# Loads of a cached-attention kernel split into two transfers of 64 partitions each

## The chip, the cores and the metric

The kernel runs on one core of one Trainium2 chip. The metric is the device time of one execution in microseconds (us), as the median of several runs; a profiled execution is one more run, of which a trace was taken. A core has a matrix engine (PE, with its weight loads shown as PEld), a vector engine (DVE), a scalar engine (ACT), GpSimd (POOL) and a sync engine (SP). SP issues the transfers between the chip's main memory (DRAM in the names) and the on-chip memory of 128 partitions; 16 DMA engines carry them out.

## What is computed

One token passes through two layers, each made of an attention block over a cache of keys and values and a mixer block, with a layer norm ahead of each. Both layers use the same weights and the same cache. Cut to what matters:

```python
def _A_ref(x, k_cache, v_cache, wq, wo):          # x: 1 x 1 x 640, 32 heads of 192
    q = (x @ wq).reshape(B, Sq, Hq, Dh).transpose(0, 2, 1, 3)
    k = k_cache[:, :, Sk - W:, :]                 # the last W = 4096 rows of 32768
    v = v_cache[:, :, Sk - W:, :]
    p = softmax(einsum("bhqd,bhkd->bhqk", q, k) * Dh ** -0.5)
    return einsum("bhqk,bhkd->bhqd", p, v).transpose(0, 2, 1, 3).reshape(B, Sq, Hq * Dh) @ wo

def _B_ref(x, w1, w2, w3, w4):                    # with one token the shifted part is zero
    x1 = x + hs
    return x1 + gelu(layernorm(x1) @ w3) @ w4

x = x + _A_ref(layernorm(x), ...)
x = x + _B_ref(layernorm(x), ...)
x = x + _A_ref(layernorm(x), ...)
x = x + _B_ref(layernorm(x), ...)
```

Everything is bfloat16. For one head, K and V are 4096 x 192 values each, 1536 KB. With a single token, every weight and cache value is used once per layer, so the work is mostly the moving of bytes: 218.5 MB are read in one execution.

## The kernel before

The 32 heads of a layer are taken in eight groups of four (`GROUPS`, L78), layer 1 from the last group to the first and layer 2 from the first to the last. For a head, `load_k` (L116) and `load_v` (L121) each bring 1536 KB into one cell: partition p gets 32 consecutive rows of the cache, 12,288 bytes in one run. `load_wo` (L137) brings the 960 KB of the output weights that belong to one group, 7,680 bytes to a partition. There are 11 cells (L72) of this size. `take` (L103) hands out the cell that has been free longest and `give` (L108) returns it when its last reader has been written into the program.

K has to be turned by DVE (`transpose_quart`, L305, instruction at L322) before PE can form the scores (`scores_quart`, L365). Layer 1 keeps the turned K of heads 0 to 6 in seven cells (`NKEEP`, L72), and layer 2 uses them without loading them again. Layer 1 also keeps half of V of head 3 (`VKEEP`, L74). In layer 2, a kept cell is given back when its head's scores are done (L511). V is read by `pv` (L450), wo by `out_proj` (L474).

The engines' order is the order in which the program is written (L89). Loads are put into one list beforehand (`layer_stream`, L174): while the V of one group comes in, the K of the next comes in turn with it, then the group's wo. SP issues the list in that order, each issue at the point where the framework's waits allow it. `need` (L210) runs the list forward as far as the load that is wanted. An issue waits for two kinds of things: for the last reader of the cell it writes, and for one of eight completion semaphores that the framework uses in turn, so that a transfer waits for the landing of the one eight places before it. Every load that is larger than a few bytes spans all 128 partitions; the last two V loads of a layer and its last wo are cut in two along the row.

The turn between the layers goes as follows. The last group of layer 1 ends at its output projection, the mixer follows with w3 (`load_w3`, L146) and w4 (`load_w4`, L154), and then attention of layer 2 begins with the scores of the kept heads 0 to 3. The V loads of heads 0 to 2 of layer 2 are issued while layer 1's mixer runs. The first K load of layer 2 is that of head 7, the next is that of head 8.

Of the kernel before, what the change touches and what calls it, by code (L numbers as in the profile page):

```python
# [17 lines left out]
P = 128  # L18
# [15 lines left out]
def kernel(  # L34
# [14 lines left out]
    nc = tc.nc  # L49
    _, _, D = A_x.shape  # L50
    _, H, Sk, Dh = A_k_cache.shape
# [9 lines left out]
    QH = 4  # L61
# [7 lines left out]
    s0 = Sk - W  # L69
# [2 lines left out]
    NKEEP, NCELL = 7, 11  # L72

    VKEEP, VHALF = 3, FREE // 2  # L74

    W3C, W4C = FREE // F, FREE // D
    assert W4C % 2 == 1 and W4C < NF
# [25 lines left out]
    def take(key):  # L103
        i = free.popleft()
        cell_of[key] = i
        return cells.tile([P, FREE], BF16, tag=f"cell{i}", name=f"cell{i}")
# [4 lines left out]
    def load_x():  # L111
        x_bf = const.tile([ND, P], BF16, name="x_bf")
        nc.sync.dma_start(x_bf[:], A_x.rearrange("a b (n p) -> (a b n) p", p=P))
        return x_bf

    def load_k(layer, h):  # L116
        t = take(("k", layer, h))
        nc.sync.dma_start(t[:], A_k_cache[0, h, s0:Sk, :].rearrange("(p j) d -> p (j d)", p=P))
        return t

    def load_v(layer, h):  # L121
        t = take(("v", layer, h))
        src = A_v_cache[0, h, s0:Sk, :].rearrange("(p j) d -> p (j d)", p=P)
        n = 2 if h in GROUPS[layer][-1][-2:] else 1
        step = FREE // n
        if (layer, h) == (1, VKEEP):
            n, step = 2, VHALF
        for i in range(n):
            if (layer, h, i) != (1, VKEEP, 0):
                nc.sync.dma_start(t[:, i * step:(i + 1) * step], src[:, i * step:(i + 1) * step])  # L130
        return t

    def load_wq(layer, kc):
# [3 lines left out]
    def load_wo(layer, c):  # L137
        t = take(("wo", layer, c))
        src = A_wo[c * QC:(c + 1) * QC, :].rearrange("(p c) n -> p (c n)", c=NA)
        n = 2 if c == GROUPS[layer][-1][0] // QH else 1  # L140
        step = NA * D // n
        for i in range(n):
            nc.sync.dma_start(t[:, i * step:(i + 1) * step], src[:, i * step:(i + 1) * step])
        return t

    def load_w3(layer):  # L146
# [7 lines left out]
    def load_w4(layer):  # L154
# [15 lines left out]
        return blocks  # L170

    LOADERS = {"x": load_x, "k": load_k, "v": load_v, "wq": load_wq, "wo": load_wo, "w3": load_w3, "w4": load_w4}

    def layer_stream(layer):  # L174
# [580 lines left out]
```

## Time and profile before

| What | Value |
|---|---|
| Median of three runs | 540.65 us (540.53 to 542.11) |
| The profiled execution's own time | 540.19 us |
| Its span, first to last instruction | 538.4 us |
| Read from DRAM | 218.53 MB, 406 GB/s over the span |
| PE busy | 281.0 us, 52% of the span |
| PEld busy | 229.0 us, 43% |
| DVE busy | 257.5 us, 48% |
| ACT busy | 54.7 us, 10% |
| Chain that ended last | DMA 71%, PE 14%, DVE 11%, issue 2%, ACT 1% |
| One issue on SP | 0.33 us |

The profile's page first gives busy times per engine, then cuts the span into 40 equal slices: in the rows of digits, 9 means busy for 90% of a slice or more, and PEclk is the clock that PE was granted, in tenths. The row of GB/s says what the DMA engines moved in each slice. The chain of waits is followed back from the last instruction, at each step to what released it; a DMA entry in it lasts from a transfer's issue to its landing, which includes the time that it stood behind earlier transfers. A table of windows gives for each stretch of time the busy time of PE, PEld, DVE, ACT and POOL with their instruction counts, the granted PE clock, the DMA engines' busy share and GB/s. DMA issues are listed with their size and the time from issue to landing.

### The profile page before, as it was taken

To read this page: it belongs to the slowest core of one execution; us is meant where nothing else is said; L and a number is where in the kernel's file an instruction comes from. 1 tells how busy PE (TensorE), PEld (TensorE's weight loads), DVE (VectorE), ACT (ScalarE), POOL (GpSimd) and SP (SyncE) were. 2 spreads that over 40 slices of the span, in tenths; PEclk is the share of its full clock that TensorE was granted. 3 is DMA by queue.
4 is the path that set the end of the run, shared out by engine and by line. 5 is a ranking of instruction groups with operands and counts; after the bars stand their busy time and mean duration, and the time that the engine had idled before them with its cause. 6 is when DMAs were issued, how large, how long until landed. Compare 5 with 4: busy or idle time off the path is not lost.

```text
span 538.4 us, 14866 instructions
## 1 busy us (share of the span) xinstructions
PE 281.0 (52%) x6820; PEld 229.0 (43%) x6820; DVE 257.5 (48%) x494; ACT 54.7 (10%) x249; POOL 2.0 (0%) x11
## 2 busy tenths in 40 slices
PE   0146546365363644545535676665454653636555
PEld 0045445254253533434425665554343543524434
DVE  2187536455455546546303147565363654545511
ACT  1001010010100101001201012010010101001011
POOL 1000000000000000000000000000000000000000
PEclk9999999999999999999999996555555555555555
DMA  8999999999999999999999999999999999999992
GB/s 351 429 422 422 419 427 421 422 424 420 421 422 425 420 422 420 421 423 425 401 401 406 345 380 424 421 421 420 424 421 424 423 420 422 424 421 424 422 408 98
DMA packets 23697, 219.48 MB, mean 408 GB/s; under 512 B 2516, under 2 KB 2900, under 8 KB 8148
## 3 DMA queue, kind: packets, MB, share of 16 engines
q1 hardware_dynamic: 23636, 218.54, 97.8%
q8 instruction: 53, 0.87, 0.7%
q14 instruction: 8, 0.07, 0.0%
HBM read 218.53 MB, written 0.00 MB: 406 GB/s over the span
## 4 chain that ended last, share of the span: by engine, by line
DMA 71%; PE 14%; DVE 11%; issue 2%; ACT 1%; SPq 0%; DVEq 0%; ACTq 0%
DVE cell_4809 L322 6%; DMA cell_567<-in_A_k_cache_dram 6%; DMA cell_1665<-in_A_v_cache_dram 5%; DMA cell_1053<-in_A_k_cache_dram 5%; DMA cell_2029<-in_A_k_cache_dram 5%; DMA cell_2517<-in_A_k_cache_dram 5%; DMA cell_3006<-in_A_k_cache_dram 5%; DMA cell_7424<-in_A_k_cache_dram 5%; DMA cell_5960<-in_A_k_cache_dram 5%; DMA cell_7917<-in_A_v_cache_dram 5%; DMA cell_6448<-in_A_k_cache_dram 5%; DMA cell_6936<-in_A_k_cache_dram 5%; PE O_ps L459 4%; DMA cell_3466<-in_A_k_cache_dram 4%; PE ST_ps L372 3%; DMA cell_8110<-in_A_wo_dram 3%
## 5 line engine op out<-in xcount | busy, mean ns | idle before, releaser
L372 PE MATMUL ST_ps<-Qblk,cell_200 128*128 128x4 bf16 x1200 | 45.6, 167 | 72.5 <-DVE cell_200 L322 72.5
L372 PE MATMUL ST_ps<-Qblk,cell_4809 128*128 128x4 bf16 x1200 | 45.3, 167 | 64.8 <-DVE cell_4809 L322 64.3
L463 DVE STREAM_TRANSPOSE o_sb<-O_ps 128x192 f32<-128x192 f32 x64 | 24.5, 383 | 113.0 <-PE O_ps L459 113.0
L459 PEld LDWEIGHTS <-PT 128*1 128x1 bf16 x2048 | 68.1, 114 | 22.8 <-issue 11.5
L372 PEld LDWEIGHTS <-cell_200 128*128 128x128 bf16 x1200 | 38.6, 105 | 85.3 <-DVE cell_200 L322 83.7
L372 PEld LDWEIGHTS <-cell_4809 128*128 128x128 bf16 x1200 | 38.5, 105 | 78.5 <-DVE cell_4809 L322 76.1
L472 ACT ACTIVATE oT<-oT_ps,rl 32x6 bf16<-32x6 f32 x64 | 16.5, 257 | 282.9 <-PE oT_ps L471 282.9
L408 ACT ACTIVATE Pr<-ST_ps,nb_sb,sc 128x32 bf16<-128x32 f32 x64 | 25.1, 487 | 0.5
L471 PE MATMUL oT_ps<-o_sb,Lq 128*32 128x6 f32 x128 | 16.9, 204 | 11.8 <-DVE o_sb L463 11.7
L339 PE MATMUL qT_ps<-xc,wq_sb 128*128 128x1 bf16 x480 | 15.8, 166 | 13.4 <-DMA wq_sb<-in_A_wq_dram 12.9
L339 PEld LDWEIGHTS <-wq_sb 128*128 128x128 bf16 x480 | 15.0, 105 | 14.1 <-DMA wq_sb<-in_A_wq_dram 13.6
L471 PEld LDWEIGHTS oT_ps<-o_sb,Lq 128*32 128x32 f32 x128 | 11.9, 141 | 20.6 <-issue 15.3
L417 PEld LDWEIGHTS <-Eq 128*32 128x32 bf16 x256 | 4.1, 105 | 31.1 <-DVE y_acc L522 25.3
L353 PE MATMUL Qrep_ps<-Xq,Lb 128*128 128x24 bf16 (+1 forms) x18 | 3.2, 180 | 24.7 <-DVE Xq L346 24.4
L408 ACT ACTIVATION_READ_ACCUMULATOR Pr<-ST_ps,nb_sb,sc 128x1 f32 x64 | 14.2, 222 | 0.0
L404 ACT COPY nb_sb<-nb_ps 128x4 f32<-128x4 f32 x16 | 2.6, 162 | 113.7 <-PE nb_ps L402 113.7
L422 PE MATMUL l_ps<-lpart,ones 128*128 128x4 f32 x32 | 9.4, 366 | 5.3 <-ACT PT L420 5.3
L346 DVE TENSOR_TENSOR Xq<-qT_ps,maskq 128x24 bf16<-128x24 f32 (+1 forms) x18 | 2.8, 155 | 19.5 <-PE qT_ps L339 19.4
L422 PEld LDWEIGHTS l_ps<-lpart,ones 128*128 128x128 f32 x32 | 8.0, 313 | 6.9 <-ACT PT L420 6.7
L402 PE MATMUL nb_ps<-dg,ones 4*128 4x4 f32 x32 | 9.0, 348 | 1.1
L402 PEld LDWEIGHTS nb_ps<-dg,ones 4*128 4x128 f32 x32 | 7.9, 307 | 1.9
L417 PE MATMUL PT_ps<-Pr,Eq 128*32 128x32 bf16 x256 | 5.3, 192 | 6.0 <-ACT Pr L408 5.8
(266 smaller groups left out, 469.2 us busy)
## 6 DMA issues: line engine op xcount, KB each, us to landing
wq_sb<-in_A_wq_dram SPq DMA_DIRECT2D x5, 1536.0 KB, 10.9
cell_198<-in_A_k_cache_dram SPq DMA_DIRECT2D x1, 1536.0 KB, 21.8
cell_256<-in_A_k_cache_dram SPq DMA_DIRECT2D x1, 1536.0 KB, 24.9
cell_317<-in_A_k_cache_dram SPq DMA_DIRECT2D x1, 1536.0 KB, 25.8
cell_371<-in_A_k_cache_dram SPq DMA_DIRECT2D x1, 1536.0 KB
cell_462<-in_A_k_cache_dram SPq DMA_DIRECT2D x1, 1536.0 KB, 30.2
cell_565<-in_A_v_cache_dram SPq DMA_DIRECT2D x1, 1536.0 KB, 30.3
cell_567<-in_A_k_cache_dram SPq DMA_DIRECT2D x1, 1536.0 KB, 30.3
```

The lines of the kernel that those rows point to most:

```text
L322: nc.vector.transpose(Tu, Ku[:, :, q * NY:(q + 1) * NY])
L339: nc.tensor.matmul(qT_ps[:, tl:tl + 1], lhsT=wq_sb[:, kc, t * P:(t + 1) * P], rhs=xc[:, kc:kc + 1], start=(kc == 0), stop=(kc == ND - 1))
L353: nc.tensor.matmul(Qrep_ps[:], lhsT=Lb[:], rhs=held["x"][:].rearrange("p t b -> p (t b)"), start=True, stop=True)
L372: nc.tensor.matmul(ST_ps[:, hq, q * ng + g, :], lhsT=T4[:, g, f, :, t], rhs=Qblk[:, h * NCOL + 2 * f + t, :], start=(n == 0), stop=(n == N ...
L402: nc.tensor.matmul(nb_ps[:], lhsT=ones[0:n, :], rhs=held["dg"][0:n, :], start=True, stop=True)
L408: nc.scalar.activation(out=Pr[:, hq].rearrange("p m g -> p g m"), in_=ST_ps[:, hq], func=ACTF.Exp, bias=nb_sb[:, hq:hq + 1], scale=sc[:, 0 ...
L417: nc.tensor.matmul(PT_ps[32 * m:32 * (m + 1), :, j, :], lhsT=Eq[:, j, :], rhs=held["Pr"][:, :, m, :], start=True, stop=True)
L422: nc.tensor.matmul(l_ps[:], lhsT=ones[:], rhs=held["l"][:], start=True, stop=True)
L459: nc.tensor.matmul(O_ps[r:r + 1, :], lhsT=PT[:, hq, i:i + 1], rhs=V[:, i * Dh:(i + 1) * Dh], start=(i < 4), stop=(i >= NB - 4))
L463: nc.vector.transpose(o_sb[:], O_ps[:].rearrange("p (a c) -> p c a", c=NA))
L471: nc.tensor.matmul(oT_ps[r, :], lhsT=Lq[:], rhs=o_sb[:, :, 0], start=True, stop=True)
L472: nc.scalar.activation(oT[r, :], oT_ps[r, :], ACTF.Copy, scale=rl[r, 0:1])
```

## The change

`load_k`, `load_v` and `load_wo` no longer issue their transfers themselves but through a new function, `start`. With `short` set, it issues two transfers, of partitions 0 to 63 and of partitions 64 to 127, one right after the other on the same queue; otherwise it issues one as before. `short` is set in layer 2 (`layer == 1` in the code) for heads under 12, that is, for K and V of the first three groups, and for those groups' wo. The bytes, the cells, the order of the loads and the instructions of the other engines stay. A run in a partition is as long as before; a half has 64 of them, four for each of 16 DMA engines, where a whole load has eight.

```diff
     VKEEP, VHALF = 3, FREE // 2
+    SHORT = 12
...
+    def start(dst, src, short):
+
+        n = P // 2 if short else P
+        for p in range(0, P, n):
+            nc.sync.dma_start(dst[p:p + n], src[p:p + n])
+
     def load_k(layer, h):
         t = take(("k", layer, h))
-        nc.sync.dma_start(t[:], A_k_cache[0, h, s0:Sk, :].rearrange("(p j) d -> p (j d)", p=P))
+        start(t[:], A_k_cache[0, h, s0:Sk, :].rearrange("(p j) d -> p (j d)", p=P), layer == 1 and h < SHORT)
         return t
...
             if (layer, h, i) != (1, VKEEP, 0):
-                nc.sync.dma_start(t[:, i * step:(i + 1) * step], src[:, i * step:(i + 1) * step])
+                start(t[:, i * step:(i + 1) * step], src[:, i * step:(i + 1) * step], layer == 1 and h < SHORT)
         return t
...
         for i in range(n):
-            nc.sync.dma_start(t[:, i * step:(i + 1) * step], src[:, i * step:(i + 1) * step])
+            start(t[:, i * step:(i + 1) * step], src[:, i * step:(i + 1) * step], layer == 1 and c * QH < SHORT)
         return t
```

## The prediction

> **What bounds the kernel now.** I read the page's slices first, then its table of DMA queues, the chain of waits in order of time, and then a table of windows over the part that the change touches.
>
> ```profile
> PEclk9999999999999999999999996555555555555555
> DMA  8999999999999999999999999999999999999992
> GB/s 351 429 422 422 419 427 421 422 424 420 421 422 425 420 422 420 421 423 425 401 401 406 345 380 424 421 421 420 424 421 424 423 420 422 424 421 424 422 408 98
> ...
> q1 hardware_dynamic: 23636, 218.54, 97.8%
> ```
>
> One slice is 538.4 / 40 = 13.46 us. The 16 DMA engines are busy from the first slice to the last but one, at 420 to 425 GB/s, and the one hardware queue q1 carries 97.8% of all engine time. The exceptions are the start, the end and slices 20 to 24 (401, 401, 406, 345, 380), the turn from layer 1 to layer 2.
>
> ```profile
> 295.37 0.25 issue
> 295.62 0.57 PE mean_ps L275 x2
> ...
> 316.81 3.45 DVE cell_4809 L322 x4
> ...
> 357.83 0.81 PE y_ps L482 x30
> 358.66 26.15 DMA cell_5960<-in_A_k_cache_dram
> ...
> 391.56 25.38 DMA cell_6448<-in_A_k_cache_dram
> ...
> 423.68 25.18 DMA cell_6936<-in_A_k_cache_dram
> ...
> 486.03 25.91 DMA cell_7917<-in_A_v_cache_dram
> ...
> 511.96 15.97 DMA cell_8110<-in_A_wo_dram
> 527.98 0.57 PE y_ps L482 x15
> ...
> 535.95 0.28 DVE o_fin L723
> ```
>
> From 295 to 358 us the chain runs over PE and DVE; from 358.66 on it is made of K and V loads, and only 8 us of arithmetic stand behind the last wo load. That compute stands in the chain from 295 to 358 doesn't make it the limit there: the next table says what the DMA does meanwhile.
>
> ```profile
> 283.00:296.00 13.00, 7.81 (x192) 7.01 (x193) 4.30 (x17) 2.20 (x10) 0.00 (x0) 1.00 1.02 403
> 296.00:309.00 13.00, 8.74 (x293) 8.49 (x294) 1.78 (x10) 0.76 (x4) 0.00 (x0) 1.00 0.96 350
> 309.00:323.00 14.00, 10.72 (x290) 9.16 (x291) 5.54 (x13) 2.26 (x11) 0.00 (x0) 1.00 0.99 377
> 323.00:358.00 35.00, 23.39 (x572) 18.76 (x564) 23.23 (x41) 4.79 (x23) 0.00 (x0) 0.56 1.01 422
> 358.00:500.00 142.00, 73.48 (x1793) 59.77 (x1791) 74.77 (x130) 13.39 (x64) 0.00 (x0) 0.50 1.01 422
> ```
>
> The last column is GB/s. From 323 on the DMA moves 422 GB/s without a gap, during the compute stretch too: it works ahead. So a microsecond of DMA time added anywhere after the turn stands in the end time, except what falls into the turn's own gaps. Those are 13 x (1 - 350/422) + 14 x (1 - 377/422) = 2.2 + 1.5 = 3.7 us between 296 and 323.
>
> [...] Every large transfer of the kernel before spans 128 partitions, so no row of its trace shows a half[...].
>
> **The change, part by part.** *Which loads.* Layer 2 doesn't load K for heads 0 to 6, which are kept transposed. The short loads are K of heads 7 to 11 (5 x 1536 KB), V of heads 0 to 11 (11 x 1536 + 768 KB, half of head 3 being kept) and wo of three groups (3 x 960 KB): 20 loads, 28,224 KB = 28.90 MB. At 422 GB/s that is 68.5 us of DMA time, from about 291 us, when the first V load gets its turn, to about 362, with the full-width K loads of heads 12 to 15 among them. On the other engines the instruction order is unchanged; on SP 20 issues become 40.
>
> *Issues.* 20 more at 0.33 us (the length of one on SP in the timeline) are 6.6 us of SP, over a stretch in which SP mostly waits. The second half's issue follows the first's, behind 1.9 us or more of transfer. Cost 0; if an engine ran dry at each, at most 6.6.
>
> *Landings.* Each half adds one packet per engine that raises the semaphore. The trace's DMA records give 9 ns for it: 20 x 9 ns = 0.2 us. The runs keep their 12 KB.
>
> *In flight.* The framework turns eight completion semaphores: a ninth transfer waits for the first. Before, that is eight loads; the landing times show it, with 28 to 31 us in the steady part, eight times 1536 KB / 422 GB/s = 3.7 us.
>
> ```profile
> cell_4807<-in_A_k_cache_dram SPq DMA_DIRECT2D x1, 1536.0 KB, 9.2
> ...
> cell_5472<-in_A_k_cache_dram SPq DMA_DIRECT2D x1, 1536.0 KB, 17.5
> ...
> cell_5861<-in_A_k_cache_dram SPq DMA_DIRECT2D x1, 1536.0 KB, 24.0
> ```
>
> In the short region landing takes 9 to 24 us, so free cells are what limits there at first. Eight halves are four loads, 15 us. SP will wait on semaphores earlier, and behind it only later issues are queued[...]. An engine still has up to seven halves, 13 us, behind the one in work. Cost 0; at most a few us if the slowest engine falls far behind.
>
> *Rate.* [...] In the records of semaphore increments around 280 us the 16 engines finish one load within 4.4 us, in two clusters of eight about 2 us apart, and inside a cluster many differ by 0.05 to 0.4 us. [...] Bounds: 1.0 (the engine's own rate is the limit[...]) and 2.0. I take 1.9[...]: 68.5 x 0.9 = 61.7 us.
>
> *What is given back.* With the engines at half pace the first V loads last until the next cells are free, so the turn's gaps close: -3.7 us. First arithmetic of layer 2 hardly waits: its V loads, issued at 286 to 295, are first read at 315.
>
> *Sum.* +61.7 - 3.7 + 0.2 = +58. The profiled execution took 540.19 us with a span of 538.4, 0.5 under the median of 540.65. It would become 598.4; against the median, 598.9. I say 598. Compute is no second limit: behind slower loads it has more time.
>
> **Rivals.** *Ports have room.* The engine's own 26.4 GB/s (422 / 16) binds, and halves run as fast as wholes. [...] Time 540.9, up to 545 if the smaller window lets engines run dry.
>
> *Half out of step.* [...] Factor 1.4: 68.5 x 0.4 - 3.7 = +24, 564. [...]
>
> *Faster.* [...] Its whole price is the 3.7 us of gaps, 537[...]. Against: both halves wait for the same cell, and that cell's release is what is late.
>
> *Worse than half.* [...] 610 and over. Nothing in the profile speaks for it.
>
> **How the numbers follow.** Likeliest, factor 1.7 to 2.0 (585 to 606 us): 0.64. Half out of step, 1.15 to 1.7 (547 to 585): 0.18. Ports have room: 0.10, of which 0.06 within 0.3% and 0.04 slower. Faster: 0.04. Worse than half: 0.04. About 0.3%, 1.6 us, is what a measurement here can tell from no change. Slower is 0.64 + 0.18 + 0.04 + 0.04 = 0.90. The range 555 to 608 takes all of the likeliest and most of the second; outside are the two cases without loss, the weak end of the second and the worst.
>
> **What would show it.** In the slices, some nine figures, from slice 20 or 21 of a longer span on, should fall to 215 to 260 GB/s with the DMA digit still at 9: engines busy but slow. The packets' time in q1 rises while the bytes stay. The chain from about 310 to 420 should be made of K and V loads in place of PE and DVE, with landings of 25 to 30 us for halves of 768 KB. After the last half the rate is 422 again and the last load is followed by the same 8 us. The prediction is wrong if the rate stays near 420 in the halves, and its reason is wrong if the time is lost with the DMA digit below 9.

## The result and the profile after

The changed kernel takes 617.78 us as the median of four runs (613.52 to 620.9), against 540.87 us before (540.53 to 542.11, four runs, one more than in the table above). The ratio is 1.141, 95% interval 1.133 to 1.150: 77 us more. The direction, the place and the halving of the rate were forecast; the size, +58 us with a range up to 608 us, was too small. The profiled execution took 620.14 us with a span of 618.0. PE was granted about half its clock in the last part of the profiled execution before and the full clock in this one, but that isn't the difference: other executions of the kernel before took 539.2 to 542.3 us at the full clock and 540.7 to 541.7 us at the lower one.

The page's slices and its row for the hardware queue, one slice being 618.0 / 40 = 15.45 us:

```profile
DMA  8999999999999999999999999999999999999992
GB/s 356 427 423 423 421 424 422 423 423 422 423 421 423 422 421 423 403 408 350 214 219 229 222 223 227 218 214 215 213 296 421 421 423 421 424 420 426 418 401 84
...
q1 hardware_dynamic: 23956, 218.54, 98.1%
```

The digits are 9 in all slices but the first and the last, as before. But for ten slices the same busy engines move 213 to 229 GB/s, about half of what they move elsewhere. The bytes of the queue are the same 218.54 MB, in 23,956 packets against 23,636: 320 more, 16 for each of the 20 added transfers.

The chain of waits, in order of time (start, length, what):

```profile
320.45 16.71 DMA cell_4990<-in_A_k_cache_dram
...
337.23 29.15 DMA cell_5290<-in_A_k_cache_dram
...
393.08 40.77 DMA cell_5785<-in_A_k_cache_dram
433.91 29.12 DMA cell_5980<-in_A_k_cache_dram
...
607.58 0.57 PE y_ps L489 x15
...
615.56 0.28 DVE o_fin L730
```

Between 320 and 358 us arithmetic stood here before; now it is K loads, with one wo load from 366 to 393 us among the later ones. Behind the last load stand 8 us of arithmetic, as before. So the difference is in the loads.

The table of windows, whose last column is GB/s:

```profile
283.00:296.00 13.00, 6.40 (x140) 5.41 (x140) 4.12 (x15) 2.22 (x10) 0.00 (x0) 1.00 1.08 299
296.00:309.00 13.00, 5.67 (x177) 5.43 (x178) 1.07 (x8) 0.30 (x2) 0.00 (x0) 1.00 1.01 215
309.00:323.00 14.00, 8.03 (x255) 7.88 (x255) 1.44 (x6) 0.97 (x5) 0.00 (x0) 1.00 1.00 220
...
320.00:380.00 60.00, 27.86 (x674) 21.90 (x671) 20.97 (x42) 5.58 (x26) 0.00 (x0) 1.00 1.02 225
...
400.00:456.00 56.00, 15.53 (x376) 12.39 (x377) 16.56 (x28) 2.79 (x13) 0.00 (x0) 1.00 1.01 215
460.00:590.00 130.00, 67.40 (x1612) 54.58 (x1613) 68.00 (x117) 13.03 (x61) 0.00 (x0) 1.00 1.01 422
...
288.00:458.00 170.00, 63.53 (x1605) 52.20 (x1601) 45.34 (x99) 11.36 (x53) 0.00 (x0) 1.00 1.02 221
```

The last row spans the slow stretch: 170 us at 221 GB/s are 37.6 MB, where 28.9 MB belong to the halves. The stretch from 400 to 456 is the telling one. In the third group every cut V stands beside a whole K of heads 12 to 15; with the wholes at full rate this row would lie well above that of the pure halves from 320 to 380. It lies below. Some 8.7 MB that were not cut seem to have gone at half rate too.

### The profile page after: what moved, and what is told of

It reads as the page before. It is cut to its first block, busy times and chain, and to the rows that moved or that the text cites. A ratio compares the mean times of both kernels' runs of the same rounds, so it can differ in the third digit from the quotient of the medians.

```text
span 618.0 us, 14898 instructions
## 1 busy us (share of the span) xinstructions
PE 283.2 (46%) x6820; PEld 229.1 (37%) x6820; DVE 257.8 (42%) x494; ACT 55.0 (9%) x249; POOL 2.0 (0%) x11
## 3 DMA queue, kind: packets, MB, share of 16 engines
q1 hardware_dynamic: 23956, 218.54, 98.1%
## 4 chain that ended last, share of the span: by engine, by line
DMA 83%; PE 7%; DVE 6%; issue 2%; ACT 1%; SPq 0%; DVEq 0%; ACTq 0%
DMA cell_5785<-in_A_k_cache_dram 7%; DMA cell_567<-in_A_k_cache_dram 5%; DMA cell_5290<-in_A_k_cache_dram 5%; DMA cell_5980<-in_A_k_cache_dram 5%; DMA cell_1665<-in_A_v_cache_dram 5%; DMA cell_1053<-in_A_k_cache_dram 5%; DMA cell_2029<-in_A_k_cache_dram 5%; DMA cell_2517<-in_A_k_cache_dram 5%; DMA cell_3006<-in_A_k_cache_dram 5%; DMA wx_sb<-in_B_w_dram 4%; DMA cell_6956<-in_A_k_cache_dram 4%; DMA cell_5484<-in_A_wo_dram 4%; DMA cell_7937<-in_A_v_cache_dram 4%; DMA cell_6468<-in_A_k_cache_dram 4%; DMA cell_7444<-in_A_k_cache_dram 4%; DMA cell_3466<-in_A_k_cache_dram 3%
## 5 line engine op out<-in xcount | busy, mean ns | idle before, releaser
L470 DVE STREAM_TRANSPOSE o_sb<-O_ps 128x192 f32<-128x192 f32 x64 | 24.4, 382 | 130.8 <-PE O_ps L466 130.8
L346 PE MATMUL qT_ps<-xc,wq_sb 128*128 128x1 bf16 x480 | 15.8, 166 | 13.4 <-DMA wq_sb<-in_A_wq_dram 12.9
L427 ACT CAST PT<-PT_ps 128x128 bf16<-128x128 f32 x16 | 4.3, 267 | 48.2 <-PE PT_ps L424 48.2
```

The source lines that it names most:

```text
L346: nc.tensor.matmul(qT_ps[:, tl:tl + 1], lhsT=wq_sb[:, kc, t * P:(t + 1) * P], rhs=xc[:, kc:kc + 1], start=(kc == 0), stop=(kc == ND - 1))
L427: nc.scalar.copy(PT[:].rearrange("p h c -> p (h c)"), PT_ps[:].rearrange("p h j g -> p (h j g)"))
L470: nc.vector.transpose(o_sb[:], O_ps[:].rearrange("p (a c) -> p c a", c=NA))
```

## What the experiments had to tell apart

The prediction's theory goes by the name *ports* in the expectations, though no record of these runs shows a port. As far as the runs can test it, it says that a transfer of 64 adjacent partitions is slow because of where these partitions lie. Its rivals were the *count* (twice as many transfers, eight completion semaphores that cover half the bytes) and the *source* (a half reads one contiguous 768 KB). Besides, the extra 19 us over the forecast needed a cause: either halves are slower than a factor of two by themselves (*own cost*), or wholes queued between them are slowed (*neighbours*). Every edit below is to the changed kernel unless another one is named. Except for the cut along the row, each version ran once; the four runs of the changed kernel itself lie between 613.5 and 620.9 us, so a few microseconds beside it decide nothing.

### Cut along the row

```diff
-        for p in range(0, P, n):
-            nc.sync.dma_start(dst[p:p + n], src[p:p + n])
+        for c in range(0, m, n):
+            nc.sync.dma_start(dst[:, c:c + n], src[:, c:c + n])
```

(m is the length of a row, n half of it for the same 20 loads.)

> The same 20 loads of layer 2 are still cut in two and issued as 40 transfers, but along the row: each spans 128 partitions, in eight runs of 6 KB for each engine in place of four of 12 KB. Bytes of each transfer, issues and turns of the eight semaphores are as in the changed kernel. Ports [...]: the loss goes, 541 us, within 2. Count (twice as many transfers, half the bytes behind eight semaphores): the loss stays, 610 to 620 us. Source (a half reads one contiguous 768 KB): the loss goes as well, since a row cut reads from all of the 1536 KB.

Measured: 542.52 us (15 runs) against 541.11 before (18 runs), ratio 1.0024, interval 1.0011 to 1.0036. The loss is gone with all 40 transfers in place, so the count isn't its cause. Its own price is small but not nothing: about 1.3 us by that ratio, for 20 more transfers and twice as many runs.

### Even and odd partitions

```diff
-        for p in range(0, P, n):
-            nc.sync.dma_start(dst[p:p + n], src[p:p + n])
+        for p in range(n):
+            nc.sync.dma_start(dst[p::n], src[p::n])
```

(n is 2 for the cut loads.)

> The same 20 loads cut in two transfers of 64 partitions with four 12 KB runs for each engine, as in the changed kernel, but the first takes the even partitions and the second the odd ones[...]. Ports: most of the loss goes, 541 to 560 us[...]. Anything that lies in 64 partitions or four runs as such, or in the count: the loss stays, 610 to 620 us.

Measured: 542.34 us in one run, beside 541.11 before. The row of GB/s on its page:

```profile
GB/s 350 429 421 423 421 425 420 422 426 420 423 422 423 419 423 423 421 424 422 403 404 390 319 356 422 421 421 422 423 423 422 421 419 423 423 421 427 419 410 107
```

It is the row of the kernel before within a few GB/s, except for the turn, where it is a little lower (319 and 356 in place of 345 and 380). Sixty-four partitions, four runs to an engine and 12 KB runs are all still there. What differs is which partitions share a transfer, and with them which rows of the cache it reads; that takes away all but about 1 us of the 77.

### One contiguous half of the source

```diff
+        if short == 2:
+            for c in range(2):
+                nc.sync.dma_start(dst[:, c * VHALF:(c + 1) * VHALF], src[c])
+            return
...
+        if layer == 1 and NKEEP <= h < SHORT:
+            start(t[:], A_k_cache[0, h, s0:Sk, :].rearrange("(c p j) d -> c p (j d)", c=2, p=P), 2)
+            return t
```

(The same for V: ten loads, K and V of heads 7 to 11. VHALF is half a row. The remaining ten are cut along the row.)

> For K and V of heads 7 to 11 each transfer reads one contiguous half of the 4096 cache rows, 768 KB, as a partition half does, but writes it to all 128 partitions (K and V of a head in the same order of rows, so the sums are the same); the other cut loads are cut along the row. Source: half of the cut loads are still slow, 570 to 585 us. Ports: no loss, 541 to 544 us.

Measured: 541.17 us, beside 540.12 before. The two experiments above both read from the whole 1536 KB with each transfer and would have hidden a cost of the source. Here half of the cut loads read as a partition half does, and nothing of the 77 us comes back. What costs is the destination.

### Quarters

```diff
-        n = P // 2 if short else P
+        n = P // 4 if short else P
```

> The 20 loads are cut into four transfers of 32 partitions, two 12 KB runs for each engine. [...] ports give the same time as halves: 611 to 622 us. A cost for each entry of an engine, or for the eight semaphores that now cover two loads, would add: 40 more transfers at 1 us or more each, 650 us and over.

Measured: 618.33 us. That lies within the 613.5 to 620.9 of the changed kernel: with the same bytes cut, transfers of 32 adjacent partitions show no other cost than those of 64. Forty further transfers and a window of two loads instead of four cost nothing that shows beside the spread of the changed kernel's own runs.

### K of heads 12 to 15 cut as well

```diff
-        start(t[:], A_k_cache[0, h, ...], layer == 1 and h < SHORT)
+        start(t[:], A_k_cache[0, h, ...], layer == 1 and h < SHORT + QH)
```

> K of heads 12 to 15 in layer 2 is cut by partitions too, so no whole load is left among the halves. Neighbours (a whole load that is queued between halves already runs at half the rate): the time stays as in the changed kernel, 613 to 621 us. Own cost (only the halves are slow, by more than a factor of two, and the wholes between them run at the full rate): four more loads of 3.73 us slow down by a factor of 1.9 to 2.2, +13 to +18 us, 627 to 638 us.

Measured: 615.66 us. Four more loads were cut and the time didn't rise. Its windows give 221 to 227 GB/s where no whole is left between the halves:

```profile
320.00:390.00 70.00, 29.38 (x708) 23.22 (x706) 24.53 (x46) 5.79 (x27) 0.00 (x0) 1.00 1.01 222
390.00:455.00 65.00, 18.95 (x444) 14.66 (x444) 17.33 (x30) 3.28 (x15) 0.00 (x0) 1.00 1.02 227
```

So the halves' own factor is 422 / 222 = 1.90 in the first row and 422 / 227 = 1.86 in the second, and the four wholes of the changed kernel had already been paid for. Neighbours, not own cost.

### K alone, alternating with whole V

```diff
-        start(t[:], A_k_cache[0, h, ...], layer == 1 and h < SHORT)
+        start(t[:], A_k_cache[0, h, ...], layer == 1 and h < 20)
...
-                start(t[...], src[...], layer == 1 and h < SHORT)
+                start(t[...], src[...], False)
```

(wo whole as well.)

> Only K of heads 7 to 19 of layer 2 is cut by partitions; V and wo stay whole, so a whole V is queued between any two cut K. 13 cut loads are 48.5 us at 422 GB/s. Own cost alone at a factor of 1.9 to 2.2: +44 to +58 us less the gaps of the turn, 581 to 597 us. Neighbours: the 13 V and 3 wo between them, some 55 us, slow down as well, +90 us, 620 to 640 us.

Measured: 624.44 us, 83.3 more than before. With fewer bytes cut than in the changed kernel (20.4 MB against 28.9) it is slower than that: 83.3 / 13 = 6.4 us for each cut load. Where all loads in a stretch are cut, it is (615.66 - 541.11) / 24 = 3.1, though four of those 24 are smaller (three wo and half a V). The time lies in the range that was given for neighbours, 620 to 640.

### Four and eight cut loads, far apart

```diff
-        start(t[:], A_k_cache[0, h, ...], layer == 1 and h < 20)
+        start(t[:], A_k_cache[0, h, ...], layer == 1 and h in range(14, 30, 4))
```

(An edit to the version above, K alone; for eight cut loads, range(12, 28, 2).)

> Only K of heads 14, 18, 22 and 26 of layer 2 is cut by partitions, with at least eight whole loads between two of them. Own cost alone: 4 x 3.4 = 13.6 us, 554 to 556 us. Neighbours within the distance that the 16 engines are apart (4 to 6 us, one or two loads): about 6 to 8 us for each cut load, 565 to 575 us. Everything in the queue slowed for as long as a half is in flight (28 us): over 600 us.

> K of the eight even heads 12 to 26 of layer 2 is cut by partitions, with three whole loads or more between two of them. Own cost alone: 8 x 3.4 = 27 us, 567 to 570 us. Neighbours within the distance of the engines: the same price for a cut load as with four of them, 6 to 8 us each, 589 to 605 us. Far reach: all wholes of the stretch, over 640 us.

Measured: 566.26 and 604.34 us beside 540.12, so 6.5 and 8.0 us for each cut load. How far one reaches is seen in the windows of the version with four, around its first two cut loads, which land at about 365 to 373 and 402 to 412 us:

```profile
340.00:360.00 20.00, 12.72 (x310) 10.39 (x299) 12.59 (x19) 2.60 (x13) 0.00 (x0) 1.00 1.01 419
360.00:376.00 16.00, 6.76 (x160) 4.89 (x158) 7.14 (x16) 0.69 (x4) 0.00 (x0) 1.00 1.01 267
376.00:396.00 20.00, 9.07 (x205) 7.31 (x206) 9.30 (x14) 0.95 (x5) 0.00 (x0) 1.00 1.01 421
398.00:414.00 16.00, 6.36 (x157) 4.92 (x156) 7.22 (x15) 0.52 (x2) 0.00 (x0) 1.00 1.02 275
416.00:434.00 18.00, 7.69 (x172) 6.03 (x162) 8.51 (x13) 0.81 (x4) 0.00 (x0) 1.00 1.01 423
```

The rate is full, low, and full again. The landing records narrow it down: each transfer raises its semaphore 16 times, which is read here as once by each of the 16 engines, and the trace has the time of each. Some engine is in the first cut load from about 361 to 373 us, some 12 us, and the rate is low about as long. That is longer than the 7.5 us that the two halves take one engine: the engines reach them at different times. The whole V ahead of this cut load takes 4.7 us on the average of the engines and the one behind it 5.0, where 3.7 is the full rate. With the 3.8 us that the halves themselves lose, that makes 6.1 of the 6.5 us that a cut load costs on average. So both neighbours pay, and loads further off do not.

In the version with eight, one engine falls back from one cut load to the next, to 21 us behind the first at 487 us, with the other fifteen within 7.3 us; and in the page's last but one slice the DMA engines are busy for only six tenths. The end waits for the slowest, which fits the higher price per load; no run tests that by itself.

### The same pattern where the engines are close together

```diff
-        start(t[:], A_k_cache[0, h, ...], layer == 1 and h < 20)
+        start(t[:], A_k_cache[0, h, ...], layer == 0 and 16 <= h < 28)
```

(An edit to the version K alone.)

> K of heads 27 to 16 is cut by partitions in layer 1 in place of layer 2, twelve loads with a whole V between any two, from the fifth K load on, where the 16 engines finish a load within 0.9 to 2.4 us of each other instead of 4 to 6. Neighbours by distance (a whole is slow while another engine is still in a half): fewer microseconds for each cut load than the 6.4 of the same pattern in layer 2, 4.4 to 5.9, so 594 to 612 us. Neighbours as such (any whole behind a half is slow): 6.4 each, 615 to 620 us. Own cost alone: 582 us.

Measured: 613.57 us, 73.5 more than before, 6.1 for each cut load: between the two expectations, and by itself no decision. The landing records say more. For each of the twelve whole V loads behind a cut K, here by the time of its issue, the table gives the mean time since the transfer before, for the first and the last eight landings, and how far first and last were apart at the transfer before:

```
V issued at    first eight   last eight   apart before
 18.40 us        4.42 us       4.83 us       2.7 us
 29.48           4.87          5.06          4.1
 42.39           4.98          5.37          4.4
 55.73           5.38          4.36          5.2   (whole wo behind it)
 72.06           5.75          6.46          6.5
 85.27           5.77          6.72          7.6
 98.29           5.94          6.79          9.0
112.60           6.17          5.36          8.8   (whole wo behind it)
130.87           6.79          6.94         10.0
143.97           6.70          7.09         10.2
158.34           6.52          7.16         10.3
172.30           6.32          4.93          9.7   (whole wo behind it)
```

A whole load takes 3.70 us in the undisturbed part of the same trace. The first one behind a half takes 4.4 to 4.8, not 7: being behind a half isn't by itself what slows it. It gets slower as the engines drift apart, and at some 10 us it is near half the full rate. Where a whole wo and no half is queued behind the V, the last eight landings come sooner. This is what one expects if a whole is slowed by engines that are still, or already, in halves. The distance itself was not set by hand, so this is a relation seen in one run and not an isolated cause.

### A forecast from these prices

```diff
-    SHORT = 12
+    SHORT = 4
```

> Only the first group is cut by partitions: V of heads 0, 1, 2, the half V of head 3 and one wo; K of head 7 stands whole among them. By the prices of the runs so far: 3 x 3.4 for the V, 3.4 for K of head 7 as a neighbour, 1.7 for the half V, 2.1 for wo, 3 at each end for wholes that overlap with halves, 3.7 less for the gaps of the turn: +20 us, 558 to 563 us. Own cost alone, without neighbours: +10 us, 549 to 553 us.

Measured: 558.45 us, +17.4 over 541.03 beside it, at the lower edge of the range of the neighbours (558 to 563) and outside that of own cost (549 to 553).

## Why the prediction was right and wrong

**Right: what bounds, and that nothing hides it.** The DMA was the limit to the end; its engines stayed busy and slow; the chain turned from arithmetic into loads from 320 to 463 us.

**Right: the size of the factor, in part by luck.** Taken: 1.9 from bounds of 1 and 2, an estimate of the author's, since no row of the trace before shows a half. In the landing records of the changed kernel a half of 768 KB takes 3.5 us where 1.86 is the full rate, 1.90. From the windows, 28.9 MB at 221 instead of 422 GB/s: 130.8 - 68.5 = 62.3 us, against 61.7 in the sum. No run shows a way from the spread of the engines, read just ahead of the 1.9, to that factor. Of the 945 packets of 12 KB that began between 330 and 385 us none took less than 0.68 us and the middle one 0.90, where 0.46 is the full rate. In this stretch every packet was slow, while the 16 landings of a transfer lay 8 to 9 us apart. Halves landed after 28.1 to 29.2 us in the middle of the stretch, where 25 to 30 was given; beside the whole K loads later on it was 30 to 42.

**Right: what is given back.** In the two windows of the turn there is no gap left (215 and 220 GB/s with the DMA busy), so the 3.7 us were returned.

**Right: the window of eight semaphores costs nothing; slightly low: the landings.** Quarters halved the window again without loss. The 0.2 us for 20 more transfers were too little for the row cut, which lost 0.6 to 1.9 us, though it also doubles the runs.

**Wrong: the step "Which loads".** It names "the full-width K loads of heads 12 to 15 among them" and gives them no cost. Even its stretch leaves them out: it ends "about 362", while in the trace before the last of the 20 loads, the third group's wo, lands at 379.8; the four K loads are 14.9 us at full rate, 3.7 each. In the landing records of the changed kernel the four take 7.1 to 7.2 us each. The bytes that went at half rate were 37.6 MB and not 28.9: the four K loads, 6.3 MB, and 2.4 MB at both ends of the stretch, the rest of w4 and the first whole loads behind. 8.7 MB at 221 instead of 422 GB/s are 39.4 - 20.6 = 18.8 us. With that term the sum is 62.3 + 18.8 - 3.7 = 77.4 us, against 77 measured. The two profiled executions themselves are 79.6 us apart by span: the time by which a given amount has been moved differs by at most 0.3 us up to 120 MB and by 77.2 us from 160 to 215 MB, and the rest comes at the very end, where the engines land 9.6 us apart in place of 6.0.

**The facts for that step were in hand.** The prediction counted engines up to 4.4 us apart, more than one whole load, and drew nothing from it for the whole loads. It didn't ask what an engine in a whole load meets while others are in halves. The rival that came nearest in time, worse than half, is wrong too: the halves by themselves lost a factor of 1.86 to 1.90, as cutting K of heads 12 to 15 shows.

**Not settled.** Why the rate halves was not shown. Shown is that it depends on which partitions a transfer takes: 64 adjacent ones ran at 221 to 227 GB/s where every load was cut, every second one of 128 at 421 to 422 behind the turn. A transfer of two separate blocks, partitions 0 to 31 with 64 to 95, was not run. That wholes beside halves go as far down as these, 7.1 us, was measured but not derived. Why the factor is 1.90 and not 2 is open too.

## What to carry to other kernels

Judge a transfer by where its partitions lie, not by how many it has: here a load that was cut along its row or into even and odd partitions cost a full queue a little over 1 us for all 20 loads (542.52 and 542.34 us against 541.11), and one cut into adjacent halves ran at about half rate (221 to 227 GB/s in place of 422). The price of a slow transfer here was not its own bytes alone: the four whole K loads between halves took 7.1 to 7.2 us each in place of 3.7. Count the neighbours as well: beside the first of four cut loads that stood far apart, the whole load ahead took 4.7 us and the one behind 5.0. Scattered cut loads cost more here, 6.1 to 8.0 us each, than cut loads in one block, 3.1.

## What the runs showed of the hardware that was not expected

A full-width transfer queued next to 64-partition ones slowed from 3.7 to as much as 7.2 us. The 16 landings of one transfer drift apart in this pattern: with K alone cut in layer 1, they grew from 2.7 to 10.3 us apart. In the changed kernel they went from 4.2 us apart to 12.9, and once the cut loads were over they came closer again, but only to 6.5. And the split into even and odd partitions, with two transfers of 64 partitions one after the other through the same queue, kept 421 to 422 GB/s behind the turn, in one run at 542.34 us.
